# Linear-memory attention and MLP on one core: from a planner's order to a written list of tasks, with score quads in segment 0

## The chip, the cores and the metric

The kernel runs on one core of one Trainium2 chip. The metric is device time in microseconds (us) of one execution, as the median of several runs. The engines are TensorE (PE in the profile; its weight loads are PEld), VectorE (DVE), ScalarE (ACT), GpSimd (POOL) and SyncE (SP). SP issues all DMAs of this kernel. Each engine works through its own instructions in the order in which they are written down; semaphores make an instruction wait for results of other engines.

## What is computed

One transformer block over 2048 tokens of width 640: `x`, `LN` without gain or bias, attention in 4 segments of 512 tokens with a memory that is carried from segment to segment, a residual, a second `LN`, and an MLP of width 1728 with SiLU, with a residual.

```python
h  = x + attention(LN(x)) @ wo          # 32 heads of 20
h2 = h + silu(LN(h) @ w1) @ w2
# in attention, for each segment s and head:
p     = softmax(qs @ ks.T * scale + causal_mask)   # within the segment
a_mem = (phi(qs) @ M) / (phi(qs) @ z + 1e-6)       # phi(t) = t + 1 if t > 0 else exp(t)
o     = g * a_mem + (1 - g) * (p @ vs)             # g = sigmoid(beta)
M += phi(ks).T @ vs ; z += sum(phi(ks))
```

## The kernel before

The kernel is written as a graph of about 1300 tasks. A task is a small piece of work for one engine: the five matmuls of one projection, the evacuation of one result, one DMA. `Graph.task` notes what a task reads and writes, and `Graph.schedule` then decides in which order tasks are emitted, which engine takes those that ScalarE or VectorE could do, and which buffer each gets. It is a planner: it steps through a modelled time, and at each step gives each free engine the ready task with the lowest priority value. The priorities come from the table `P`. Where TensorE has no ready task, the planner puts in a filler, a matmul of zeros (L738). The `Tracker` then turns the emitted order into instructions with semaphore waits.

Per segment `s` (0 to 3) the tasks are these, with the lines of their instructions:

- Layer norm of 4 blocks of 128 tokens: statistics on VectorE (L841, L844), the reciprocal square root of the variance on POOL in two small steps (L850, L852), the normalisation on VectorE (L858). For the first four blocks TensorE transposes the result (L868), ScalarE or VectorE copies it to `nT` (L877, L878); all other blocks are transposed by a DMA (L883).
- V for 4 blocks (L910) and its evacuation (L920 on ScalarE, L921 on VectorE).
- Q and K as 5 chunks each (L938), evacuated to `QK` (L948 ScalarE, L949 VectorE). For the memory: the exponential of it (L956, ScalarE) and `phi` (L963, L966, VectorE). Chunks hold 4 heads per 32 partitions; 12 of the 32 heads are spread over the gaps of the chunks and are put together in `QKV` by 16 small DMAs (L977).
- The memory update from `phi(k)`, transposed by DMA (L1162), on TensorE (L1170), then VectorE or ScalarE (L1196, L1199) and POOL (L1206).
- 8 "ticks", each for a group of 4 heads: scores (L1018), exponentials (L1029, ScalarE, two banks per instruction), the causal mask on POOL (L1040), attention times V (L1068), its evacuation `oTs` (L1084, VectorE), the turn back to tokens and the memory's part (L1100, L1104), and the division (L1117 to L1137, VectorE; L1145, POOL).
- The back part: `otok` transposed by DMA (L1230), the product with `wo` (L1238), the residual (L1246), the second layer norm, 14 chunks of the hidden layer (L1266, and L1261 for the half chunk), SiLU by a tanh (L1280, ScalarE) and a product (L1285, VectorE), in segment 3 by one SiLU (L1274, ScalarE), the second product (L1326, L1301 for the last block), the second residual (L1336, L1311) and the output's DMA.

PSUM has two pools of four banks: `ps` (`ps_gen`) for nearly everything, `sc` (`ps_sc`) for scores. Scores use the array as four row tiles: the four heads of a group lie on 4 x 32 partitions, each with its own bank. There are 20 score groups per segment (per tick A and B, and one E for two ticks). `QUAD_SEGS` tells in which segments the four heads of a group are one task (a quad, all four `sc` banks); in the others they are two tasks of two heads (pairs, two banks each):

```python
QUAD_SEGS = (1, 2, 3)
for r0, nr in ([(0, 4)] if quad else [(0, 2), (2, 2)]):
    sca = G.alloc("sc", nr)
```

An exponential reads two banks, so a quad is read out by two of them and a pair by one. A `ps` buffer of two banks was always a neighbouring pair that begins at an even bank.

Of the kernel before, what the change touches and what calls it, by code (L numbers as in the profile page):

```python
# [210 lines left out]
class Alloc:  # L211
    __slots__ = ("pool", "size", "slot", "users", "last_write", "reads", "turn", "lock")

    def __init__(self, pool, size=1):
        self.pool = pool
        self.size = size
        self.slot = None
        self.users = 0
        self.lock = 0.0
        self.last_write = {}  # L220
        self.reads = {}

    def keys(self, subs):
        if self.pool in ("ps", "sc"):
            return [(self.pool, self.slot + i) for i in range(self.size)]
        return [(self.pool, self.slot, s) for s in subs]


class Task:
    __slots__ = ("name", "engs", "emit", "reads", "writes", "prio", "mode", "allocs", "preds", "npred",  # L230
                 "succ", "ready", "lat", "start", "end", "eng", "idx", "bw")
# [6 lines left out]
class Graph:  # L238
    def __init__(self, pools):
# [3 lines left out]
        self.flex = P["flex"]  # L243
        self.filler = None
        self.fill_from = 1.0
        self.start_at = 0.75
        self.fill_all = 12.0
        self.fill_to = 400.0
        self.free_order = ("x", "ps", "ex", "th", "st", "xn", "rd")

    def alloc(self, pool, size=1):
        a = Alloc(pool, size)
        a.turn = self.turns.get(pool, 0)
        self.turns[pool] = a.turn + 1
        return a

    def task(self, name, engs, emit, reads=(), writes=(), prio=0.0, mode=None, reserve=(), lat=None, bw=0.0):

        t = Task()
        t.name, t.engs, t.emit, t.prio, t.mode, t.lat, t.bw = name, engs, emit, prio, mode, lat, bw  # L260
# [31 lines left out]
    def schedule(self):  # L292
        import heapq
        tasks = self.tasks
        for t in tasks:
            t.succ = []
            t.npred = len(t.preds)
            t.ready = 0.0
            t.start = t.eng = None
        for t in tasks:  # L300
            for p in t.preds:
                tasks[p].succ.append(t.idx)
        free = {p: [True] * n for p, n in self.pools.items()}
        events = []
        engfree = {e: self.start_at for e in ENGS}
        pemode = [None]
        WIN = 3.4133
        busy = {}
        rate = {0: 0.5}

        def pe_rate(t):
            w = int(t / WIN)
            for v in range(max(rate), w):
                rate[v + 1] = 1.0 if busy.get(v, 0.0) >= 0.39 * WIN else 0.5
            return rate[w]

        def pe_busy(st, en, r):
            w = int(st / WIN)
            while st < en:
                e2 = min(en, (w + 1) * WIN)  # L320
                busy[w] = busy.get(w, 0.0) + (e2 - st) * r
                st = e2
                w += 1
        dmaq = [0.0]
        cand = {e: [] for e in ENGS}
        order = []
        left = len(tasks)

        def push(t):
            for e in t.engs:  # L330
                cand[e].append(t.idx)

        turn = {p: 0 for p in self.pools}

        def find(a):
            f = free[a.pool]
            if a.pool not in self.free_order and a.turn != turn[a.pool]:
                return None
            if a.size == 1:
                if a.pool == "ps":  # L340
                    n = len(f)
                    for i in range(n):
                        if f[i] and not f[i ^ 1]:
                            return i
                for i, x in enumerate(f):
                    if x:
                        return i
                return None
            for i in range(0, len(f), a.size):
                if all(f[i:i + a.size]):  # L350
                    return i
            return None

        def can(t):
            need = [a for a in t.allocs if a.slot is None]
            if not need:
                return True
            taken = []
            ok = True
            for a in need:  # L360
                i = find(a)
                if i is None:
                    ok = False
                    break
                for k in range(a.size):
                    free[a.pool][i + k] = False
                taken.append((a, i))
            for a, i in taken:
                for k in range(a.size):
                    free[a.pool][i + k] = True  # L370
            return ok

        def fill_ok(t):
            return t > self.fill_from and t < self.fill_to and (
                t < self.fill_all or busy.get(int(t / WIN), 0.0) < P["fill"] * WIN)

        now = self.start_at
        for t in tasks:
            if t.npred == 0:
                push(t)  # L380
        done_heap = []
        rel_heap = []
        while left:
            progressed = True
            hold = []
            while progressed:
                progressed = False
                for e in ENGS:
                    if engfree[e] > now + 1e-9:
                        continue  # L390
# [113 lines left out]
D = 640  # L504
# [892 lines left out]
```

## Time and profile before

| | |
|---|---|
| Median of 3 runs | 314.56 us (313.83 to 314.69) |
| Profiled execution | 313.93 us, of which 312.0 us span |
| TensorE busy | 300.4 us (96% of the span), 2719 matmuls |
| ScalarE busy | 212.0 us (68%) |
| VectorE busy | 220.2 us (71%) |
| POOL busy | 150.2 us (48%) |
| Granted TensorE clock | 1.00 throughout |

The span runs from the first to the last instruction of the program. "Busy" is the time in which at least one instruction of that engine is under way. A group's row gives line, engine, operation, what is written and read with shapes, the count, then busy time, the mean of one in ns, and the engine's idle time just before such instructions with what ended it. A chain's row gives start, length, engine, tile and line. A timeline's row gives start, length, engine, line, operation, shapes and count, and in brackets the idle time before it and who ended it. A stretch's row gives its bounds, its length, then the busy time of PE, PEld, DVE, ACT and POOL, each with a count of instructions, then the granted clock, DMA share and GB/s; for one line alone only the engines that it uses.

### The profile page before, as it was taken

To read this page: it belongs to the slowest core of one execution; us is meant where nothing else is said; L and a number is where in the kernel's file an instruction comes from. 1 tells how busy PE (TensorE), PEld (TensorE's weight loads), DVE (VectorE), ACT (ScalarE), POOL (GpSimd) and SP (SyncE) were. 2 spreads that over 40 slices of the span, in tenths; PEclk is the share of its full clock that TensorE was granted. 3 is DMA by queue.
4 is the path that set the end of the run, shared out by engine and by line. 5 is a ranking of instruction groups with operands and counts; after the bars stand their busy time and mean duration, and the time that the engine had idled before them with its cause. 6 is when DMAs were issued, how large, how long until landed. Compare 5 with 4: busy or idle time off the path is not lost.

```text
span 312.0 us, 6863 instructions
## 1 busy us (share of the span) xinstructions
PE 300.4 (96%) x2719; PEld 161.6 (52%) x2719; DVE 220.2 (71%) x454; ACT 212.0 (68%) x273; POOL 150.2 (48%) x292
## 2 busy tenths in 40 slices
PE   8999999988999999999999999999999999999996
PEld 6543543445644345565545454456654446664574
DVE  5649978895799889989897857993765695920012
ACT  2889999985669899878677678986568932005400
POOL 7879745652565546545476634654454431300000
PEclk9999999999999999999999999999999999999999
DMA  7657617755469300623150212332110004330001
GB/s 219 204 159 160 96 26 200 181 141 81 83 115 244 111 2 1 99 48 67 44 120 2 61 33 40 57 42 65 40 47 21 2 2 85 79 70 21 2 32 53
DMA packets 51103, 24.61 MB, mean 79 GB/s; under 512 B 39680, under 2 KB 49792, under 8 KB 51072
## 3 DMA queue, kind: packets, MB, share of 16 engines
q1 hardware_dynamic: 51072, 24.19, 34.9%
q8 instruction: 21, 0.34, 0.5%
q14 instruction: 10, 0.08, 0.1%
HBM read 10.41 MB, written 2.62 MB: 42 GB/s over the span
## 4 chain that ended last, share of the span: by engine, by line
PE 63%; DVE 14%; ACT 7%; POOL 5%; SPq 4%; DMA 4%; issue 3%; DVEq 0%; ACTq 0%
PE ps_gen L1326 17%; PE ps_gen L1266 10%; PE ps_gen L938 8%; PE ps_gen L1238 6%; PE ps_sc L1018 5%; PE ps_sc L1266 4%; PE ps_gen L1068 4%; SPq L977 3%; PE ps_gen L910 3%; ACT PTB L1029 3%; DVE on L1137 2%; DVE stt L841 2%; ACT PTA L1029 1%; DMA sT<-in_A_wq_dram 1%; PE ps_gen L1170 1%
## 5 line engine op out<-in xcount | busy, mean ns | idle before, releaser
L1029 ACT ACTIVATE PTA<-ps_sc 128x1024 bf16<-128x1024 f32 x64 | 63.0, 1033 | 14.9 <-PE ps_sc L1018 14.8
L1029 ACT ACTIVATE PTB<-ps_sc 128x1024 bf16<-128x1024 f32 x64 | 62.9, 1037 | 13.6 <-PE ps_sc L1018 13.5
L1326 PE MATMUL ps_gen<-w_sb,sT 128*128 128x320 bf16 x420 | 60.3, 299 | 0.3 <-DVE on L1137 0.3
L1040 POOL TENSOR_SCALAR_AFFINE_SELECT PTB<-PTB 128x512 bf16<-128x512 bf16 x64 | 41.5, 648 | 36.7 <-ACT PTB L1029 34.5
L1326 PEld LDWEIGHTS ps_gen<-w_sb,sT 128*128 128x128 bf16 x420 | 39.8, 98 | 18.5 <-issue 1.9
L1266 PE MATMUL ps_gen<-nT,w_sb 128*128 128x512 bf16 x195 | 46.7, 380 | 1.6 <-DVE sT L1285 1.4
L1029 ACT ACTIVATE PTE<-ps_sc 128x1024 bf16<-128x1024 f32 x32 | 31.1, 1031 | 8.3 <-PE ps_sc L1018 8.3
L1285 DVE SCALAR_TENSOR_TENSOR sT<-th,ps_gen 128x512 bf16<-128x512 f32 (+1 forms) x42 | 27.3, 661 | 10.7 <-ACT th L1280 10.2
L1040 POOL TENSOR_SCALAR_AFFINE_SELECT PTA<-PTA 128x512 bf16<-128x512 bf16 x32 | 21.0, 657 | 23.5 <-ACT PTA L1029 23.5
L1280 ACT ACTIVATE th<-ps_gen 128x512 f32<-128x512 f32 (+1 forms) x42 | 24.6, 593 | 10.1 <-PE ps_gen L1266 6.7
L1336 DVE SCALAR_TENSOR_TENSOR x_tok<-ps_gen,x_tok 128x640 bf16<-128x640 f32 x15 | 12.3, 820 | 24.6 <-PE ps_gen L1326 24.6
L841 DVE BATCH_NORM_STATS2 stt<-x_tok 128x6 f32<-128x320 bf16 x64 | 27.8, 476 | 2.4 <-DMA x_tok<-in_A_x_dram 2.3
L1266 PEld LDWEIGHTS ps_gen<-nT,w_sb 128*128 128x128 bf16 x195 | 17.4, 98 | 22.3 <-DVE sT L1285 3.2
L1040 POOL TENSOR_SCALAR_AFFINE_SELECT PTE<-PTE 128x512 bf16<-128x512 bf16 x32 | 20.6, 644 | 14.6 <-ACT PTE L1029 13.4
L949 DVE CAST QK<-ps_gen 128x512 bf16<-128x512 f32 x33 | 22.3, 680 | 7.5 <-PE ps_gen L938 7.5
L1145 POOL TENSOR_TENSOR otok<-on 128x320 bf16<-128x320 bf16 x24 | 19.2, 799 | 14.8 <-DVE on L1137 13.9
L1274 ACT ACTIVATE sT<-ps_sc 128x512 bf16<-128x512 f32 (+1 forms) x14 | 8.2, 582 | 26.6 <-PE ps_sc L1266 26.5
L1084 DVE TENSOR_SCALAR oTs<-ps_gen,lsc 128x512 bf16<-128x512 f32 x32 | 23.8, 743 | 3.4 <-PE ps_gen L1068 3.3
L938 PE MATMUL ps_gen<-nT,wqr 128*128 128x512 bf16 x100 | 25.0, 381 | 0.5 <-DVE QK L949 0.3
L938 PE MATMUL ps_gen<-nT,wkr 128*128 128x512 bf16 x100 | 25.0, 380 | 0.0
L910 PE MATMUL ps_gen<-wv_sb,nT 128*128 128x320 bf16 x160 | 24.1, 300 | 0.2 <-DVE on L1137 0.2
L1238 PE MATMUL ps_gen<-wo_sb,oT 128*128 128x320 bf16 x160 | 23.9, 299 | 0.4 <-DVE rd L1131 0.2
(98 smaller groups left out, 455.9 us busy)
## 6 DMA issues: line engine op xcount, KB each, us to landing
x_tok<-in_A_x_dram SPq DMA_DIRECT2D x16, 160.0 KB, 2.6
out_dram<-x_tok SPq DMA_DIRECT2D x15, 160.0 KB, 1.8
w_sb<-in_B_w_dram SPq DMA_DIRECT2D x5, 432.0 KB, 3.7
w_sb<-in_B_w_dram SPq DMA_DIRECT2D x6, 320.0 KB, 4.3
QKV<-QK SPq DMA_DIRECT2D x16, 72.0 KB
sT<-in_A_wq_dram SPq DMA_DIRECT2D x2, 400.0 KB, 5.1
sT<-in_A_wk_dram SPq DMA_DIRECT2D x2, 400.0 KB, 5.7
wv_sb<-in_A_wv_dram SPq DMA_DIRECT2D x1, 800.0 KB, 7.8
```

Of the source, the lines that this page charges most:

```text
L841: T.add(DV, lambda e, hh=hh: e.bn_stats(out=stt[:, s, 6 * hh:6 * hh + 6], in_=xb[:, 320 * hh:320 * hh + 320]), reads=R((xa, xsub)), writes ...
L910: fns.append(lambda e, c=c, hh=hh: e.matmul(bank(ps, hh)[:, 0:320], lhsT=xT[:, c, 128 * i:128 * i + 128], rhs=wv_sb[:, c, :].rearrange("p ...
L938: fns = [lambda e, kc=kc: e.matmul(bank(ps), lhsT=wt[:, kc, c, :], rhs=xT[:, kc, :], start=(kc == 0), stop=(kc == NC - 1)) for kc in range ...
L949: (lambda e: e.tensor_copy(out=o, in_=bank(ps)))
L1029: T.add(AC, lambda e: e.activation(out=pt[:, pta.slot, q0:q0 + 2, :], in_=sc3[:, b0:b0 + 2, :], func=ACT.Exp, scale=SCALE), reads=[("sc", ...
L1040: fns.append(lambda e, v=v: e.affine_select(out=v, in_=v, pattern=[[0, 4], [1, 128]], compare_op=ALU.is_ge, fill=0.0, base=0, channel_mult ...
L1084: f = lambda e: e.tensor_scalar(out=oTs[:, ots.slot, :], in0=bank(po), scalar1=lsc[:, g:g + 1], scalar2=None, op0=ALU.mult)
L1238: fns.append(lambda e, c=c, hh=hh: e.matmul(bank(ps, hh)[:, 0:320], lhsT=oT[:, c, 128 * i:128 * i + 128], rhs=wo_sb[:, c, 320 * hh:320 * h ...
L1266: fns = [lambda e, c=c: e.matmul(bank(ps), lhsT=w1_sb[:, c, 128 * f:128 * f + 128], rhs=hT[:, c, :], start=(c == 0), stop=(c == NC - 1)) f ...
L1280: T.add(AC, lambda e: e.activation(out=th[:, tha.slot, 0:nt], in_=bank(ps)[:, 0:nt], func=ACT.Tanh, scale=0.5), reads=R((ps, [0])), writes ...
L1285: T.add(DV, lambda e: e.scalar_tensor_tensor(out=sT[:, f, 0:nt], in0=th[:, tha.slot, 0:nt], scalar=1.0, in1=bank(ps)[:, 0:nt], op0=ALU.add ...
L1326: fns.append(lambda e, f=f, hh=hh: e.matmul(bank(ps, hh)[:, 0:320], lhsT=s_of(i, f), rhs=w2_of(i, f, 320 * hh), start=(f == 0), stop=(f == ...
```

## The change

- The planner is gone. `ORDER` lists all 1313 tasks by number in the order in which they are placed, `ENGINE` gives each task's engine by a letter, and `BANK` the first `ps` bank of each result. `schedule` places them one after the other at the earliest time its model allows, takes other buffers as they come free, and sorts by start. The order on each engine is therefore another one throughout, SP's too.
- Fillers are put in only before 12 us of the modelled time, and only while TensorE waits there.
- Segment 0 is in `QUAD_SEGS`: its scores are quads like the others.
- Two-bank results that are evacuated through `pair` (V, `wo`, the second product, L1100/L1104) may lie in any two banks, also not neighbours.
- In the first layer norm of the first four blocks, the statistics of block 1 come from ScalarE: one pass that copies the block and sums it, one that squares its distance from the mean and sums that, each followed by a small product with 1/640 on POOL. The other three stay on VectorE.
- The reciprocal square root of these four blocks is taken for two blocks at a time (POOL, 128x2 in place of 128x1), and their normalisations follow it.
- The load of the first weights: K's half before Q's. Blocks 8 to 11 of `x` are loaded early.
- In the order of the whole, ScalarE does 11 of the 32 `oTs` evacuations (none before) and 11 of the 40 `QK` evacuations (7 before).

The diff, cut to its core:

```diff
-QUAD_SEGS = (1, 2, 3)
+QUAD_SEGS = (0, 1, 2, 3)
 NPE = 2
 TP_SC = (1, 2)
+ST_ACT = (1,)
...
+ORDER = [
+    51, 47, 0, 1, 49, 113, 50, 46, 48, 114, 115, 116, 112, 3, 2, 125, 5, 124, 117, 118, 119, 4, 121, 122, 7, 120, 126,
...
+ENGINE = (
+    "sssssssssssssssssssssssssssssssgssssssssssssssgggggdgggdagddadgdgggggggggggggggggggggggggggggdgdgada"
...
+BANK = (
+    "0200022113320210200133110120332021100222010001003121033002202210213030021313310101222202203230202020"
...
     def schedule(self):
-        import heapq
         tasks = self.tasks
...
+        for idx in ORDER:
+            t = tasks[idx]
+            e = t.eng
+            st = free[e]
+            for p in t.preds:
+                p = tasks[p]
+                st = max(st, p.end if e == PE and p.eng == PE else p.ready)
...
+            if e == PE:
+                if st < self.fill_all:
+                    fill(max(free[PE], self.fill_from), st)
...
+        order.sort(key=lambda t: t.start)
...
     def pair(a):
-        return flat(a).rearrange("p (b x) -> p b x", b=2)
+        i, j = a.banks
+        return ps_all[:, :].rearrange("p (b x) -> p b x", b=4)[:, i:j + 1:j - i, :]
...
+        def e_sum(eng):
+            s = st.slot + j
+            T.add(AC, lambda e: e.activation(out=xn_rot[:, xn.slot, :], in_=x_tok[:, b, :], func=ACT.Identity,
+                                             accum_out=stt[:, s, 0:1]),
+                  reads=R((xa, xsub)), writes=R((st, [f"s0{j}"]), (xn, [0])))
+
+        def e_sq(eng):
+            s = st.slot + j
+            T.add(AC, lambda e: e.activation(out=xn_rot[:, xn.slot, :], in_=x_tok[:, b, :], func=ACT.Square,
+                                             scale=-1.0, bias=mvt[:, s, 0:1], accum_out=stt[:, s, 1:2]),
+                  reads=R((xa, xsub), (st, [f"m{j}"])), writes=R((st, [f"s1{j}"]), (xn, [0])))
...
+        if early and b in ST_ACT:
+            G.task(f"{tag}sa{b}", {AC: act_c(640) + 0.1}, e_sum, [(xa, xsub)], [(st, [f"s0{j}"]), (xn, [0])], prio)
+            part("sm", 0, f"m{j}")
+            G.task(f"{tag}sq{b}", {AC: act_c(640) + 0.1}, e_sq, [(xa, xsub), (st, [f"m{j}"])],
+                   [(st, [f"s1{j}"]), (xn, [0])], prio)
+            part("sv", 1, f"v{j}")
...
         def e_rstd(eng):
-            s = st.slot
-            T.add(PO, lambda e: e.tensor_tensor(out=rst[:, s, :], in0=mvt[:, s, 1:2], in1=eps_c[:, 0:1], op=ALU.add),
-                  reads=R((st, ["mv"]), (C, ["eps"])), writes=R((st, ["r"])))
...
+            r, v = rst[:, st.slot:st.slot + n, 0], mvt[:, st.slot:st.slot + n, 1]
+            T.add(PO, lambda e: e.tensor_tensor(out=r, in0=v, in1=eps_c[:, 0:1].to_broadcast([128, n]), op=ALU.add),
+                  reads=R((st, vs), (C, ["eps"])), writes=R((st, ["r"])))
```

More of the change, by code (lines that the diff above doesn't have):

```diff
@@ L325, in schedule @@
[L325 to L352, printed above, removed]
@@ new lines, in schedule @@
+        banks = iter(BANK)
+        for t, e in zip(tasks, ENGINE):
+            t.eng = dict(p=PE, a=AC, d=DV, g=PO, s=SP)[e]
+            for a in t.allocs:
+                if a.pool == "ps" and a.banks is None:
+                    i = int(next(banks))
+                    a.banks = list(range(i, i + a.size))
+        order = []
+        rel = {p: [0.0] * n for p, n in self.pools.items()}
+        held = {p: [False] * n for p, n in self.pools.items()}
+        turn = {p: 0 for p in self.pools}
```

388 lines of the change are left out of this document (175 added, 213 removed), and 71 rows, old and new, of tables (ORDER, P).

## The prediction

> **What bounds the kernel now.** I read the page first (engine totals, then the chain that ended last), then stretches, then single instructions.
>
> ```profile
> PE 300.4 (96%) x2719; PEld 161.6 (52%) x2719; DVE 220.2 (71%) x454; ACT 212.0 (68%) x273; POOL 150.2 (48%) x292
> ...
> PE 63%; DVE 14%; ACT 7%; POOL 5%; SPq 4%; DMA 4%; issue 3%; DVEq 0%; ACTq 0%
> ```
>
> TensorE is the bound, yet "96%" does not mean that nothing is left. A matmul's recorded time includes its way through the array, which overlaps the next one. So I count from start to start, with prices from the chain in order of time:
>
> ```profile
> 48.14 1.08 PE ps_gen L938 x5
> 49.22 0.32 PE ps_sc L1018 x2
> 49.54 1.19 PE ps_gen L938 x5
> 50.72 0.46 PE ps_sc L1018 x6
> 51.19 1.19 PE ps_gen L938 x5
> 52.37 0.32 PE ps_sc L1018 x4
> 52.69 0.66 PE ps_gen L1068 x16
> ...
> 267.91 11.41 PE ps_gen L1326 x84
> 279.32 1.73 PE ps_sc L1266 x8
> ```
>
> A 512-column matmul takes 0.216 us (1.08 / 5, 1.73 / 8) and a 320-column one 0.136 (11.41 / 84). Five matmuls that end in a change of array shape, from full to row-tiled scores (L1018), take 1.19 instead of 1.08, so a change costs about 0.1 us.
>
> ```profile
> 11.06 1.24 PE L938 MATMUL ps_gen<-nT,wkr 128*128 128x512 bf16 x5
> ```
>
> Segment 0 runs from this first projection (11.06) to the first score of segment 1 (66.73); the rest goes to the end of the last matmul.
>
> ```profile
> 11.03:66.72 55.69, 54.53 (x475) 25.16 (x473) 43.61 (x105) 52.96 (x72) 38.98 (x91) 1.00 0.59 139
> 66.72:309.41 242.69, 236.83 (x2178) 129.78 (x2177) 168.37 (x330) 153.98 (x194) 102.23 (x172) 1.00 0.28 57
> ```
>
> The columns are length, then busy time of PE, PEld, DVE, ACT, POOL. In segment 0 ScalarE (52.96 of 55.69) is as full as TensorE; later TensorE stands alone (ACT 153.98 of 242.69). Counting the rest at the prices above: 360 matmuls of 512 columns 77.8, 688 of 320 columns 93.6, 292 small ones 14.5, 25 groups of L1068, 60 of scores and 4 half-wide, with their changes of shape, 45.5. The largest groups of that stretch are
>
> ```profile
> L1326 PE MATMUL ps_gen<-w_sb,sT 128*128 128x320 bf16 x420 | 60.3, 299 | 0.3 <-DVE on L1137 0.3
> L1266 PE MATMUL ps_gen<-nT,w_sb 128*128 128x512 bf16 x195 | 46.7, 380 | 1.6 <-DVE sT L1285 1.4
> ```
>
> That is 231.4 us of work in 242.7: TensorE waits some 11.3 us there (13 filler matmuls lie inside). The same count of segment 0 gives 53.6 us of work and 2.1 of waits.
>
> **The change, part by part.** The build's order has the same real matmuls, 17 fewer fillers (46, none after the start) and 202 changes of array shape instead of 219.
>
> *Scores of segment 0 by quads.* Before, each of its 20 score groups is two pairs, mostly with other work between; afterwards one quad.
>
> ```profile
> 14.60:66.72 52.12, 12.85 (x128) 3.93 (x128) 1.00 0.61 142
> 66.72:247.20 180.48, 23.76 (x384) 6.68 (x384) 1.00 0.31 62
> ```
>
> These are the L1018 instructions alone. Segments 1 to 3 need 23.76 / 60 = 0.396 us per group, so 20 groups would be 7.9 busy instead of 12.85. Part of the 4.9 is array delay that the next matmul hides; from start to start it is 8.1 against 4.7, a gain of 3.4, which I take (bounds 3 to 4.9). The 17 fewer changes of shape give 17 x 0.1 = 1.6 to 1.7. Sum of both: -5.0.
>
> *What the quad costs.* A quad fills all four score banks, so the next cannot start before both exponentials of this one are read out. The tightest such loop, on PE and then on ACT:
>
> ```profile
> 164.26 0.29 PE L1018 MATMUL ps_sc<-QK 20*128 20x256 bf16 x4
> 164.38 0.28 PE L1018 MATMUL ps_sc<-QKV 20*128 20x256 bf16 x4
> 164.59 1.53 PE L1238 MATMUL ps_gen<-wo_sb,oT 128*128 128x320 bf16 x10
> 165.96 0.33 PE L1100 MATMUL ps_gen<-Mzb,phiQ 128*128 128x96 bf16 x4
> 166.13 0.33 PE L1104 MATMUL ps_gen<-sel,oTs 128*128 128x96 bf16 x4
> 166.70 0.40 PE L1018 MATMUL ps_sc<-QKV 20*128 20x512 bf16 x4 [0.24 <-ACT PTE L1029]
> ```
>
> ```profile
> 140.48 1.67 ACT L956 ACTIVATE ex<-QK 128x512 bf16<-128x512 bf16 x3
> ...
> 164.71 1.94 ACT L1029 ACTIVATE PTE<-ps_sc 128x1024 bf16<-128x1024 f32 x2 [0.68 <-PE ps_sc L1018]
> 167.15 1.02 ACT L1029 ACTIVATE PTA<-ps_sc 128x1024 bf16<-128x1024 f32 x1 [0.50 <-PE ps_sc L1018]
> ```
>
> From quad to quad at least 2.44 us pass (164.26 to 166.70). I summed what TensorE has between consecutive quads of the new segment 0: in 11 of 20 places less than that, 22.7 us together where 11 x 2.44 = 26.8 are needed. So TensorE waits 4.2 us there for ScalarE. One more ACT instruction per loop (0.52: three L956 end 1.67 after the first begins, one alone takes 0.63) fits the 0.5 us in which ACT waits for the scores; one place has three, 0.3 more. The Trainium skill ("TensorEngine Tiling (Array Packing)", Gotcha 1: PSUM Pressure) says that different row tiles write to different PSUM banks. By that rule a quad must take four, and the loop agrees: the quad at 166.70 starts 0.05 us after ACT has left the banks.
>
> *The start.* On VectorE before:
>
> ```profile
> 7.06 0.21 DVE L844 BATCH_NORM_AGGREGATE mvt<-stt 128x2 f32<-128x12 f32 x1
> 7.21 1.31 DVE L858 TENSOR_SCALAR xn_rot<-x_tok,mvt,rst 128x640 bf16<-128x640 bf16 x3
> 8.45 0.19 DVE L753 TENSOR_SCALAR sel<-iot 128x96 bf16<-128x96 int32 x1
> 8.79 0.71 DVE L858 TENSOR_SCALAR xn_rot<-x_tok,mvt,rst 128x640 bf16<-128x640 bf16 x1 [0.15 <-POOL rst L852]
> 9.42 0.81 DVE L878 CAST nT<-ps_sc 128x640 bf16<-128x640 f32 x1
> 10.15 0.81 DVE L878 CAST nT<-ps_gen 128x640 bf16<-128x640 f32 x1
> ```
>
> Statistics of four blocks end at 7.27, the last normalisation (behind POOL's rstd) at 9.50, the last copy at 10.96, and the first projection follows at 11.06. With block 1 on ScalarE, VectorE has its three blocks done about 1.0 earlier, and the second pair's rstd should be out near 7.6. Four normalisations of 0.44 then end near 8.6, one weight copy and one L878 near 9.9; first projection about 10.1. I take -1.0 (bounds -0.3, if block 1's two ACT passes and four small POOL steps come late, and -1.4). The new list then has the first score right after both projections, where before V work stood between: TensorE must wait 0.7 for the evacuation.
>
> *Segment 0 together.* Work 53.6 becomes 49.65 (scores -3.4, 14 fewer changes of shape -1.35, three memory products pulled in, one small step moved out). From 10.1: 49.65 + 0.7 + 4.2 + 0.3 + 0.7 for other waits = 65.6, where before stood 66.73. So -1.1: the quads nearly pay for themselves in waits.
>
> *The rest.* Work falls by 1.1 (what segment 0 pulled in, three changes fewer). Of the 11.3 of waits, some 2.9 stand at 66.7 to 74.6, around the end of segment 0, ending with
>
> ```profile
> 74.57 0.50 PE L1170 MATMUL ps_gen<-Vx,phiKt 128*128 128x192 bf16 x4 [1.04 <-DMA phiKt<-phiK]
> ```
>
> That transpose was issued on SP behind seven L977 copies; in the new SP order it stands ahead of all of segment 1's. Most of the other 8.4 end with a VectorE evacuation. The new list gives ScalarE 11 of the 32
>
> ```profile
> L1084 DVE TENSOR_SCALAR oTs<-ps_gen,lsc 128x512 bf16<-128x512 f32 x32 | 23.8, 743 | 3.4 <-PE ps_gen L1068 3.3
> ```
>
> and four more L949 copies, some 11 us off VectorE. Bounds: all of 8.4 stay or grow by half (rigid lists can hold an evacuation behind something late), or nearly all go. I take 4.7. New ones: 1.2 where TensorE's work between quads is under 2.44 (segment 3), and 0.9 before the last segment's first product: before, three blocks' second product (the 11.41 row) covered layer norm and transposes there, now two (7.6). Waits 11.3 -> 6.8, so -4.5, and with the work -5.6.
>
> *Sum.* The profiled execution took 313.93 (span 312.0 and 1.93 around it; the median of the runs is 0.63 above). 313.93 - 1.1 - 5.6 = 307.2; I say 307.0. The same by parts: start -1.0, work -5.0, waits 13.4 -> 12.7.
>
> **Rivals.**
> *The waits do not shrink.* The fixed list only shifts them and the VectorE part stays at 8.4: 307 + 3.7 = 310.7; with half as much again 315. For: the distance from the last attention output product to the next segment's first hidden product shrinks to 7 or 8 us of TensorE work everywhere. Against: less VectorE load. Chance 0.2, of it 0.05 at no change.
> *The quad loop decides (slower).* Place: segment 0's loop on ScalarE. The 24 other ACT instructions between its exponentials hide in no gap: 24 x 0.52 = 12.5 on 20 x 2.44 = 48.8, the first exponential at about 13.5, so segment 1 starts near 75 instead of 65.6, and the kernel takes 316. It decides from about 0.29 us exposed per instruction. For: ACT has 52.96 of 55.69 there already. Against: the row at 167.15, where ACT idled 0.50 inside the loop. By that page of the Trainium skill (Gotcha 1: PSUM Pressure) taken alone the result would be this one, since a quad that takes a bank for each row tile has no second buffer here. Chance 0.09, and 0.05 for a late list elsewhere that gives the same.
> *The loop waits cost nothing extra.* The 4.2 absorb other waits and VectorE is quick: 302 to 303. Chance 0.1.
>
> **How the numbers follow.** Forecast (303 to 310.5) 0.56, the rivals as given. A difference under 0.3% (0.9 us) can't be told from none here. Faster: 0.56 + 0.1 + 0.15 = 0.81; same 0.05; slower 0.14. The range 301 to 315 leaves out part of the slow rivals and the lowest waits.
>
> **What would show it.** Right: L1018 busy near 7.9 in segment 0, ACT's loop there near 2.44 to 2.6 per quad with TensorE waiting there for the exponentials, first projection near 10.1, segment 1's first score near 65.6, fewer TensorE waits on VectorE later. Wrong: first exponential later than 15, segment 1's first score after 68, or TensorE waits over 13 us after it, above all on LN chains and DMA transposes.

## The result and the profile after

The changed kernel takes 312.20 us (median of 15 runs, 310.33 to 316.14) where the kernel before takes 314.55 (15 runs, 313.83 to 315.48): a ratio of 0.9926 with a 95% interval of 0.9902 to 0.9950. Run again on another chip, beside the kernel before, it took 312.47 us, ratio 0.9938 (0.9913 to 0.9962). So it is faster by some 2 us, less than a third of the 7 us forecast. The ratios leave out single runs over 1.5% above their kernel's fastest (316.14 here, one each in two of the variants below), the medians do not.

The profiled execution took 312.17 us, of which 310.3 are span. First the engine totals and the chain by engine, from the changed kernel's page:

```profile
PE 291.9 (94%) x2674; PEld 159.4 (51%) x2702; DVE 214.1 (69%) x435; ACT 223.5 (72%) x291; POOL 150.0 (48%) x293
...
PE 67%; ACT 12%; DVE 9%; DMA 6%; issue 3%; SPq 1%; POOL 0%; POOLq 0%; ACTq 0%; DVEq 0%
```

The 291.9 are too low: 28 matmuls lack a record (2674 of 2702; the weight loads are complete, and all 28 have 512 columns). With these put back TensorE is busy about 295.5 us, 5.0 us less than before (300.4), and that is still 95% of the span, which is only 1.7 us shorter. ScalarE's place on the chain grows from 7% to 12%, VectorE's falls from 14% to 9%. Nine of the profiles told of here, this one among them, lack such records, and in all nine the first matmul of the first projection is one of them. Times of the first projection and waits are given below with these matmuls put back, counted from start to start at 0.216 us each; recorded rows are shown as they are.

Now the two stretches, cut at the first recorded matmul of the first projection (the real first one began at 11.62) and at segment 1's first score, columns as before:

```profile
11.82:69.18 57.36, 50.53 (x473) 24.86 (x478) 48.55 (x109) 51.91 (x69) 41.65 (x101) 0.99 0.57 130
69.18:307.70 238.52, 231.77 (x2136) 127.66 (x2156) 158.67 (x310) 166.28 (x214) 102.41 (x172) 0.99 0.29 60
```

Segment 0 became longer, 57.6 (from 11.62) for 55.7, although TensorE, with the matmuls put back, is busy about 3.0 us less in it; the rest became 4.2 us shorter. The scores of segment 0 alone (L1052, before L1018):

```profile
14.60:69.18 54.58, 7.92 (x128) 2.26 (x128) 0.99 0.55 120
```

7.92 busy for 12.85: as forecast. The start, from the timeline:

```profile
3.08 0.89 DVE L828 BATCH_NORM_STATS2 stt<-x_tok 128x6 f32<-128x320 bf16 x2 [2.02 <-DMA x_tok<-in_A_x_dram]
5.71 0.89 DVE L828 BATCH_NORM_STATS2 stt<-x_tok 128x6 f32<-128x320 bf16 x2 [1.49 <-DMA x_tok<-in_A_x_dram]
9.09 1.21 DVE L878 TENSOR_SCALAR xn_rot<-x_tok,mvt,rst 128x640 bf16<-128x640 bf16 x2 [0.59 <-POOL rst L870]
11.61 0.33 PEld L971 LDWEIGHTS ps_gen<-nT,wkr 128*128 128x128 bf16 x3 [0.20 <-ACT nT L900]
11.84 0.38 PE L971 MATMUL ps_gen<-nT,wkr 128*128 128x512 bf16 x1
```

VectorE stands idle for 1.49 us until the third block of `x` has landed. The row at 11.84 is the first projection's second matmul; the first, whose weights are loaded at 11.61, left no record, so the projection comes at about 11.62. In segment 0 two places stand out. Around 50 us (SP's rows are the issues of DMAs):

```profile
45.07 0.44 SPq L651 DMA_DIRECT2D w_sb<-in_B_w_dram  x1
45.56 1.20 SPq L1196 DMA_TRANSPOSE phiKt<-phiK  x1
46.81 0.59 SPq L651 DMA_DIRECT2D w_sb<-in_B_w_dram  x1
47.44 1.19 SPq L1196 DMA_TRANSPOSE phiKt<-phiK  x1
...
52.62 0.66 PE L1204 MATMUL ps_gen<-Vx,phiKt 128*128 128x288 bf16 x4 [1.36 <-DMA phiKt<-phiK]
```

The memory product of chunk 3 waits for a transpose issued 5.2 us earlier, right behind a weight load of 432 KB. And at the segment's end:

```profile
65.48 0.90 DVE L878 TENSOR_SCALAR xn_rot<-x_tok,mvt,rst 128x640 bf16<-128x640 bf16 x1
66.30 0.34 DVE L1233 TENSOR_TENSOR Mz<-ps_gen,Mz 128x192 f32<-128x192 f32 x1
66.70 0.40 PE L1102 MATMUL ps_gen<-PTA,Vx 128*32 128x512 bf16 x4 [0.75 <-DVE Mz L1233]
67.53 0.49 DVE L1153 TENSOR_TENSOR otok<-ps_gen,rd 128x320 bf16<-128x320 f32 x1
68.17 0.77 PE L1204 MATMUL ps_gen<-Vx,phiKt 128*128 128x192 bf16 x4 [0.74 <-DVE otok L1153]
69.19 0.61 PE L1052 MATMUL ps_sc<-QK 20*128 20x512 bf16 x4
```

TensorE waits twice for PSUM banks that VectorE empties late, the first time behind a layer-norm apply ("apply" is the normalisation of one block, L878). Right after, its clock is halved; a stretch of the changed kernel, clock in the third column from the end:

```profile
68.22:71.63 3.41, 3.41 (x28) 1.89 (x32) 2.18 (x6) 2.67 (x4) 2.00 (x3) 0.50 0.58 131
```

Last, the largest wait of the rest, near 92 us:

```profile
91.89 0.45 DVE L878 TENSOR_SCALAR xn_rot<-x_tok,mvt,rst 128x640 bf16<-128x640 bf16 x1 [1.35 <-DMA nT<-xn_rot]
92.25 0.69 DVE L982 CAST QK<-ps_gen 128x512 bf16<-128x512 f32 x1
...
92.99 0.34 PE L1134 MATMUL ps_gen<-Mzb,phiQ 128*128 128x96 bf16 x4 [1.16 <-DVE QK L982]
```

VectorE itself stands still for 1.35 us in an apply, whose buffer a transpose is still reading; the evacuation of a `QK` tile is queued behind it, and TensorE waits for that tile's bank.

### The profile page after: what moved, and what is told of

Same layout as the page of the kernel before. It is cut to its first block, busy times and chain, and to the rows that moved or that the text cites. A ratio compares the mean times of both kernels' runs of the same rounds, so it can differ in the third digit from the quotient of the medians.

```text
span 310.3 us, 6823 instructions
## 1 busy us (share of the span) xinstructions
PE 291.9 (94%) x2674; PEld 159.4 (51%) x2702; DVE 214.1 (69%) x435; ACT 223.5 (72%) x291; POOL 150.0 (48%) x293
## 4 chain that ended last, share of the span: by engine, by line
PE 67%; ACT 12%; DVE 9%; DMA 6%; issue 3%; SPq 1%; POOL 0%; POOLq 0%; ACTq 0%; DVEq 0%
PE ps_gen L1360 16%; PE ps_gen L971 10%; PE ps_gen L1300 9%; PE ps_sc L1052 6%; PE ps_gen L943 5%; PE ps_gen L1102 5%; PE ps_sc L1300 4%; PE ps_gen L1272 4%; ACT PTB L1063 4%; ACT PTA L1063 3%; ACT th L1314 2%; DMA nT<-xn_rot 2%; PE ps_gen L1134 2%; DVE stt L828 2%; PE ps_gen L1204 2%
## 5 line engine op out<-in xcount | busy, mean ns | idle before, releaser
L1063 ACT ACTIVATE PTB<-ps_sc 128x1024 bf16<-128x1024 f32 x64 | 62.1, 1022 | 9.4 <-PE ps_sc L1052 9.2
L1360 PE MATMUL ps_gen<-w_sb,sT 128*128 128x320 bf16 x420 | 61.4, 299 | 0.6 <-DVE x_tok L1280 0.6
L1300 PE MATMUL ps_gen<-nT,w_sb 128*128 128x512 bf16 x185 | 45.1, 380 | 1.3 <-DVE sT L1319 0.5
L828 DVE BATCH_NORM_STATS2 stt<-x_tok 128x6 f32<-128x320 bf16 x62 | 27.0, 477 | 3.8 <-DMA x_tok<-in_A_x_dram 3.5
L982 DVE CAST QK<-ps_gen 128x512 bf16<-128x512 f32 x29 | 19.8, 684 | 7.9 <-PE ps_gen L971 7.9
L971 PE MATMUL ps_gen<-nT,wkr 128*128 128x512 bf16 x93 | 23.2, 379 | 1.0 <-issue 0.8
L971 PE MATMUL ps_gen<-nT,wqr 128*128 128x512 bf16 x91 | 22.8, 379 | 1.1 <-issue 0.7
L1370 DVE SCALAR_TENSOR_TENSOR x_tok<-ps_gen,x_tok 128x640 bf16<-128x640 f32 x15 | 12.4, 824 | 16.1 <-PE ps_gen L1360 15.8
L1052 PE MATMUL ps_sc<-QK 20*128 20x256 bf16 (+3 forms) x320 | 20.4, 304 | 2.4 <-ACT PTA L1063 1.1
```

The source lines that it names most:

```text
L828: T.add(DV, lambda e, hh=hh: e.bn_stats(out=stt[:, s, 6 * hh:6 * hh + 6], in_=xb[:, 320 * hh:320 * hh + 320]), reads=R((xa, xsub)), writes ...
L971: fns = [lambda e, kc=kc: e.matmul(bank(ps), lhsT=wt[:, kc, c, :], rhs=xT[:, kc, :], start=(kc == 0), stop=(kc == NC - 1)) for kc in range ...
L982: (lambda e: e.tensor_copy(out=o, in_=bank(ps)))
L1052: fns.append(lambda e, j=j, o=o, n=n, r=r, qa=qa, ka=ka: e.matmul(sc_all[:, o:o + n], lhsT=ka[32 * r:32 * r + DH, 128 * j:128 * j + 128], ...
L1063: T.add(AC, lambda e: e.activation(out=pt[:, pta.slot, q0:q0 + 2, :], in_=sc3[:, b0:b0 + 2, :], func=ACT.Exp, scale=SCALE), reads=[("sc", ...
L1300: fns = [lambda e, c=c: e.matmul(bank(ps), lhsT=w1_sb[:, c, 128 * f:128 * f + 128], rhs=hT[:, c, :], start=(c == 0), stop=(c == NC - 1)) f ...
```

## The experiments

The table gives each one's median, its ratio to the kernel before on the same chip, and from its profile: first projection; from there to segment 1's first score; from there to the end of the last matmul. (The expectations go by the recorded 11.84 and 57.35 of the changed kernel, which are 11.62 and 57.57 here.) Line numbers in the rows of some variants are 1 or 3 higher than in the changed kernel.

| kernel | us | ratio (95%) | start | segment 0 | rest |
|---|---|---|---|---|---|
| before | 314.55 | 1 | 11.06 | 55.67 | 242.60 |
| changed | 312.20 | 0.9926 (0.9902 to 0.9950) | 11.62 | 57.57 | 238.43 |
| changed, again | 312.47 | 0.9938 (0.9913 to 0.9962) | 11.26 | 58.45 | 239.57 |
| two loads behind transposes | 308.03 | 0.9807 (0.9784 to 0.9829) | 10.82 | 57.76 | 235.84 |
| LN apply later | 310.49 | 0.9870 (0.9834 to 0.9905) | 10.81 | 57.15 | 238.84 |
| pairs in segment 0 | 310.94 | 0.9888 (0.9868 to 0.9909) | 10.45 | 58.72 | 237.77 |
| statistics on VectorE | 310.54 | 0.9868 (0.9847 to 0.9890) | 10.95 | 56.99 | 238.00 |
| evacuation first | 309.66 | 0.9848 (0.9821 to 0.9875) | 11.09 | 56.94 | 236.29 |
| three loads behind transposes | 308.89 | 0.9831 (0.9810 to 0.9852) | 11.08 | 58.02 | 236.39 |
| three moves together | 310.63 | 0.9878 (0.9858 to 0.9897) | 10.39 | 56.33 | 238.95 |
| load order of before | 311.25 | 0.9898 (0.9874 to 0.9921) | 11.31 | 57.22 | 237.52 |
| loads spread, two moves | 308.29 | 0.9796 (0.9767 to 0.9825) | 10.64 | 55.34 | 236.40 |
| the same with pairs | 308.54 | 0.9791 (0.9760 to 0.9823) | 11.12 | 54.48 | 236.85 |
| rstd one block at a time | 311.19 | 0.9899 (0.9872 to 0.9925) | 11.12 | 56.73 | 239.29 |
| beta ahead of the weights | 312.46 | 0.9946 (0.9916 to 0.9976) | 13.86 | 59.21 | 236.95 |

The theory after reading the trace: three kinds of waits ate the gain, each with its own cause (SP's order, VectorE's order, the loads at the start). The rival: the quad loop paces segment 0, so that a wait removed comes back elsewhere.

**The changed kernel once more**, no edit.

> The changed kernel itself once more, on the chip that the next three use, as their yardstick. Theory (its first profile fell on a late landing of the third block of x and on the half-clock stretch, both by chance): the third block lands before 5.2 us, the first projection comes at 10.8 and not at 11.84, and the median is 310.5 to 312.2, above the run with kt03 first (308.0) by 2 us or more. Rival (the late landing belongs to the order of the loads): the third block lands at 5.5 or later again and the first projection comes at 11.5 or later.

Measured: VectorE's second pair of statistics starts at 5.27, the first projection at 11.26, median 312.47. Neither expectation fits fully: landing and start lie between them, the start nearer to the rival. Two rows of its timeline, around 50 us and around 230 us, tell how much the same program moves from execution to execution:

```profile
53.57 0.67 PE L1204 MATMUL ps_gen<-Vx,phiKt 128*128 128x288 bf16 x4 [2.20 <-DMA phiKt<-phiK]
```

```profile
233.34 1.02 PE L1300 MATMUL ps_gen<-nT,w_sb 128*128 128x512 bf16 x4 [1.72 <-DMA nT<-xn_rot]
```

The first is the wait of 1.36 from above; the second has no counterpart in the first profile (there 0.1 us). This one, for the last layer-norm transpose ahead of segment 2's hidden layer, was 1.7 to 2.0 us from start to start in 4 of 13 profiles of changed kernels and at most 0.5 in the other 9.

**Two weight loads behind the transposes.**

```diff
 L651 load of w_sb, 432 KB
 L1196 transpose of phiK, chunk 2
-L651 load of w_sb, 432 KB
 L1196 transpose of phiK, chunk 3
-L651 load of w_sb, 320 KB
 L1196 transpose of phiK, chunk 4
+L651 load of w_sb, 432 KB
+L651 load of w_sb, 320 KB
```

> The changed kernel with two weight loads of the feed-forward moved on SyncE behind the transposes of phiK of chunks 3 and 4 (nothing else). Theory (the wait was real loss): the memory product of chunk 3, which stood idle 1.36 us for its transpose in the changed kernel's trace (50.87 to 52.57), waits under 0.3 us, segment 1's first score comes at 67.8 instead of 69.19, and the time falls by 1.4 us to 310.8 (ratio to the kernel before 0.988). Rival (the quad loop paces segment 0): the idle time turns up before the next score tile, segment 1's first score stays within 0.3 us of 69.2, and the time stays at 312.2 (0.9926).

Measured: 308.03 us, the fastest median of all, but not for the reason given. Its timeline around 50 us:

```profile
45.70 7.37 SPq L1196 DMA_TRANSPOSE phiKt<-phiK  x3
...
51.27 0.50 PE L1204 MATMUL ps_gen<-Vx,phiKt 128*128 128x192 bf16 x4 [1.37 <-DMA phiKt<-phiK]
```

Now chunk 2's product waits 1.37 us, and segment 0 is no shorter (57.76). What was gained lies elsewhere: a start at 10.82, no half clock, and no wait near 90 us (from segment 1's third tick to its fourth 7.98 us instead of 9.21). The last came by accident: VectorE has no wait of its own in the apply there. The likely reason, not shown, is that the moved loads shifted the modelled times by which `place` takes buffers, so that this apply got a buffer that nobody was reading.

**The evacuation ahead of the waiting apply**, which does the same on purpose.

```diff
-L878 apply (waits for a transpose to have read its buffer)
 L982 evacuation of segment 2's first QK tile
+L878 apply
```

> The changed kernel with one VectorE instruction moved: the evacuation of segment 2's first QK tile (L982) ahead of the LN apply that waits for a transpose to have read its buffer. Theory (the wait of 1.23 to 1.55 us before L1134 at 90 to 92 us, released by that evacuation, is VectorE's order): it falls below 0.2 us and the time falls by 1.2 to 1.5 against the changed kernel run beside it. Rival (the LN apply, now later, delays the transposed blocks and the work that reads them): the wait is gone but its time turns up within the next 40 us and the time stays within 0.4 us.

Its timeline near 89 us:

```profile
88.79 0.69 DVE L982 CAST QK<-ps_gen 128x512 bf16<-128x512 f32 x1 [0.28 <-PE ps_gen L971]
...
89.67 0.34 PE L1134 MATMUL ps_gen<-Mzb,phiQ 128*128 128x96 bf16 x4
```

L1134 no longer waits, and that step takes 7.98 us. The time fell by 2.8 us against the changed kernel beside it (309.66 to 312.47), more than the 1.2 to 1.5 that this wait explains. The part beyond that isn't shown to be the edit's: the profile with the edit also drew smaller waits at 50 us (0.83) and 230 us (0.1), and full clock.

**The LN apply of block 9 later.**

```diff
-L878 apply of block 9
 L1233 memory add; L1151, L1153 normalisation; L1151, L1153 normalisation
+L878 apply of block 9
```

> The changed kernel with one VectorE instruction moved: the LN apply of block 9 (0.90 us at 65.48) stands behind the memory add and the two normalisations that TensorE waits for (L1233, twice L1151 and L1153), instead of ahead of them. Theory (VectorE's order makes the waits at the end of segment 0, and these the half clock): the waits of 0.75 and 0.74 us before L1102 at 66.70 and L1204 at 68.17 fall below 0.4 us together, the half-clock stretch of 3.41 us goes or shrinks, the mean clock is 1.000, and the time falls by 1.1 for the waits and by up to 1.7 for the clock, to 309.4 to 311.1, with a smaller spread. Rival (another release is next in line): the waits move to the memory products of chunks 2 and 3, segment 1's first score stays at 69.2, and the time is 312.2.

Its timeline at the end of segment 0:

```profile
65.33 0.34 DVE L1233 TENSOR_TENSOR Mz<-ps_gen,Mz 128x192 f32<-128x192 f32 x1
65.73 0.40 PE L1102 MATMUL ps_gen<-PTA,Vx 128*32 128x512 bf16 x4
...
66.57 0.49 DVE L1153 TENSOR_TENSOR otok<-ps_gen,rd 128x320 bf16<-128x320 f32 x1
67.20 0.49 PE L1204 MATMUL ps_gen<-Vx,phiKt 128*128 128x192 bf16 x4 [0.74 <-DVE otok L1153]
```

The first of the two waits is gone, the second is as long as it was: half of the expectation. The clock was 1.000 in 5 of 6 runs. The time fell by 1.7 to 2.0 us, of which 0.75 is the wait. The rest can't be put down to the edit: the variant with VectorE's statistics, which keeps both waits, came out at 310.54 too.

**Three loads behind the transposes.**

```diff
-L651 load of w_sb, 432 KB
 L1196 transpose of phiK, chunk 2
-L651 load of w_sb, 432 KB
 L1196 transpose of phiK, chunk 3
-L651 load of w_sb, 320 KB
 L1196 transpose of phiK, chunk 4
+L651 load of w_sb, 432 KB
+L651 load of w_sb, 432 KB
+L651 load of w_sb, 320 KB
```

> The changed kernel with three weight loads of the feed-forward (432, 432 and 320 KB) moved on SyncE behind the transposes of phiK of chunks 2 to 4. In the run that moved two of them, the memory products waited 1.44 us all the same, with the first load still ahead. Theory (the loads ahead slow the transposes): without any load ahead the transpose of chunk 2 lands within 3 us of its issue, the wait before L1204 at 50 us falls below 0.4 us, and segment 0 (first projection to segment 1's first score, 57.35 us in the changed kernel's trace) shortens by 1 us or more. Rival (the transposes come too late since SyncE's 16 copies to QKV, 0.65 to 0.69 us each, end at 45.2, and two transposes share the queues): the wait stays above 1 us.

Its timeline from 51 us on:

```profile
51.11 1.53 SPq L651 DMA_DIRECT2D w_sb<-in_B_w_dram  x3
...
58.77 1.27 SPq L1196 DMA_TRANSPOSE phiKt<-phiK  x1
...
59.80 0.50 PE L1204 MATMUL ps_gen<-Vx,phiKt 128*128 128x192 bf16 x4 [1.84 <-DMA phiKt<-phiK]
```

The wait at 50 us is gone, so the loads ahead had made it. But the three loads now stand ahead of the next chunk's transpose, and its product waits 1.84 us. Segment 0 gains nothing (58.02); in this profile the clock is also at half from 61.01 to 64.42, behind that wait.

**The three moves together** (the three loads, the apply of block 9, the evacuation).

> The three moves together: the three weight loads behind the transposes, the LN apply of block 9 behind the normalisations, and segment 2's first evacuation ahead of the LN apply. Theory (the waits are independent): the gains add up to 4 to 5 us against the changed kernel run beside it, 306 to 307.5 (ratio to before 0.974 to 0.980), and the clock stays at 1.000. Rival (the quad loop of 2.45 to 2.5 us paces segment 0 and only the later move counts): 309 to 310.

Measured: 310.63, outside of both. Segment 0 fell to 56.33, with a wait of 1.5 us left behind the three loads, and the rest drew the wait near 230 us (1.7). Only 4 runs; why it stands above its parts isn't settled.

**The loads spread, with the two VectorE moves.** One load behind the transpose of block 8, one ahead of that of block 10, three behind the transposes of `otok`.

> The changed kernel with the weight loads taken off every transpose of phiK of segment 0: one of 432 KB behind the transpose of block 8, one where another stood before block 10, three behind the transposes of otok; and the two VectorE moves of the runs before. Theory (each wait in the first 92 us has its own cause, and the sum of three moves failed since the loads were put ahead of the next chunk's transposes): no wait for a transpose of phiK over 0.5 us is left, segment 1's first score comes 54.5 to 55.5 us after the first projection (57.35 in the changed kernel, 56.1 with the three moves), and the time is 306.5 to 308.5. Rival (the loads only move the wait on again): another wait of 1.5 to 2 us for a transpose appears between 80 and 110 us and the time is 309 to 310.5.

No product waits for a transpose of `phiK` any more, segment 0 takes 55.34, and the time is 308.29: as expected, and with the next kernel the best ratio of all. It beats the changed kernel by 1.3% and the kernel before by 2.0%.

**Pairs in segment 0**, once in the changed kernel and once in the one just told.

```diff
-QUAD_SEGS = (0, 1, 2, 3)
+QUAD_SEGS = (1, 2, 3)
```

with the second pair of each group in `ORDER` right behind the first.

> The changed kernel with segment 0's scores by pairs again: each quad is two pairs, one right behind the other in the quad's place, so that no shape change is added; all else is the same. Theory (quads save TensorE time as the prediction had it, and the loop costs a part of it): TensorE's work grows by 2.5 to 3.4 us, the waits of segment 0 shrink by 1 to 1.5 because the first exponential starts half a tile earlier, and the time is 313.5 to 315 (0.996 to 1.001). Rival (the quad loop of 2.45 us paces segment 0 and eats the saving): segment 1's first score comes no later than 69.2 and the time is 311 to 312.5.

> The kernel of the run beside it (loads spread, two VectorE moves) with segment 0's scores by pairs, one pair right behind the other in the quad's place. Theory (quads are worth their TensorE work, 1.2 us for 4.67 against 5.86 us of score products, and no more, since the exponentials pace the loop either way): the time is 0.8 to 1.6 us above the run beside it. Rival (the earlier first exponential pays for the work): equal within 0.5 us or faster.

The first came out at 310.94 (ratio 0.9888), below both expectations and not slower than the changed kernel; its segment 0 was long (58.72), with the wait at 50 us and a half clock from 53.39 to 56.80 in it, and its start early, so it can't decide. The second can, since the waits for transposes are out of the way. The stretch of segment 0, columns as before and both cut at the first recorded matmul, first of the kernel with quads:

```profile
10.85:65.97 55.12, 50.09 (x473) 24.60 (x478) 47.67 (x108) 50.85 (x68) 40.92 (x99) 1.00 0.48 114
```

and of the same with pairs:

```profile
11.33:65.59 54.26, 51.25 (x473) 25.38 (x478) 48.27 (x108) 50.20 (x68) 40.84 (x99) 1.00 0.49 114
```

With pairs TensorE is busy 1.2 us longer, and the segment is 0.9 us shorter. Counted from start to start, score work is 6.09 instead of 4.67, and the waits for exponentials are 0.87 instead of 2.96. The times are equal (308.54 and 308.29). So the rival holds: in this order quads are worth nothing that could be measured over adjacent pairs. ScalarE is busy 50 to 51 of 54 to 55 us in either, which fits a segment that it paces; but TensorE is as full, so that isn't shown.

**Statistics of block 1 on VectorE** (`ST_ACT = ()`), **rstd one block at a time, the load order of before.**

```diff
-ST_ACT = (1,)
+ST_ACT = ()
```

> The changed kernel with the LN statistics of block 1 back on VectorE (between those of blocks 0 and 3); the pairs for rstd and the load order stay. Theory (the late start came from the late landing of the third block, 5.69 us, which is chance of the loads): the first projection comes at 10.9 to 12.0 depending on that landing alone, no earlier than with ScalarE's statistics at the same landing, and the time is within 0.5 us of 312.2. Rival (statistics by ScalarE are what made the start late, by the accumulator reads and the extra products): with VectorE's statistics the first projection comes at 10.9 or earlier also with a late landing, and the time falls by 0.8 to 311.4.

> The changed kernel with rstd of blocks 0 to 3 one block at a time again (four pairs of GpSimd instructions of 128x1 instead of two of 128x2); statistics by ScalarE, load order and the number of fill products stay. Theory (a pair waits for the later of its two blocks): rstd of block 3 is ready 1 us earlier, its apply and transposes run ahead of those of block 2, and the first projection comes 0.2 to 0.5 us earlier at the same landing of x (that is at the landing of the third block's statistics plus 5.7, against plus 6.1 in four of the traces so far); the time falls by as much. Rival (GpSimd's extra starts cost as much): the first projection comes no earlier than landing plus 6.0.

> The changed kernel with the first eight loads in the order of the kernel before (blocks 0, 1, 2, 3 of x, then w_q ahead of w_k in both halves), VectorE's statistics of blocks 2 and 3 in that order, and no more fill products than the changed kernel has. In the trace of before the packets of the four blocks had ended at 4.44 us, in six traces with the changed order at 4.86 to 5.99. Theory (the order makes the weights' packets overtake the last of x): the four blocks have landed by 4.6, the first projection comes at 10.0 to 10.6, and the time falls by 0.7 to 1.2 against the changed kernel (312.2 to 312.5). Rival (chance of the queues): they end at 4.8 or later again, the first projection comes at 10.8 to 11.8, the time is unchanged.

With all statistics on VectorE, those of its first three blocks run without a gap (its timeline), and the first projection comes at 10.95:

```profile
3.07 0.89 DVE L828 BATCH_NORM_STATS2 stt<-x_tok 128x6 f32<-128x320 bf16 x2 [2.00 <-DMA x_tok<-in_A_x_dram]
4.12 0.83 DVE L828 BATCH_NORM_STATS2 stt<-x_tok 128x6 f32<-128x320 bf16 x2
5.11 0.83 DVE L828 BATCH_NORM_STATS2 stt<-x_tok 128x6 f32<-128x320 bf16 x2
```

VectorE does block 1 in the time that it otherwise waits for the third block. In the 11 profiles with ScalarE's statistics and paired rstd the first projection lies at 10.39 to 11.62 (mean 10.96), some 5.6 to 6.3 us behind the start of the third block's statistics. Rstd by single blocks gave 5.7 where eight of those eleven gave 5.8 to 6.3: the pair costs perhaps 0.2 us. The load order of before did not land `x` earlier (last packet at 5.50, first projection 11.31): chance, not the order. All three times (310.54, 311.19, 311.25) lie 1 to 2 us below the changed kernel's, more than their starts (10.95, 11.12, 11.31) account for; that part isn't explained.

**The kernel before, two more profiles, and beta ahead of the weights.**

> The kernel before once more, for its trace. Theory (the loads of x land later in the changed kernel by something the change did): the packets of the four blocks of x have ended by 4.5 us again (4.44 in its first trace; 4.86 to 5.99 in ten traces of changed kernels, the one with before's load order among them), and the first projection comes at 11.0. Rival (chance): they end at 4.8 or later and the first projection comes at 11.3 or later.

> The same kernel as in the look before it, for a second draw, with the same expectations: packets of x ended by 4.5 us (theory) or at 4.8 us or later (chance).

> The kernel with the loads spread and the two VectorE moves (308.29 us, ratio 0.9796), with the two loads of beta ahead of the first weight load on SyncE, so that the weights are issued 0.9 to 1.8 us later. Theory (weight packets overtake the last packets of x, which end at 5.29 there, and the start hangs on those): the blocks of x have landed by 4.5, the first projection comes at 9.9 to 10.4 instead of 10.86, and the time falls by 0.5 to 0.9 to 307.4 to 307.8. Rival (the weights, now later, take over as what the first projection waits for): the first projection comes at 10.8 or later and the time does not fall.

The packets of `x` ended at 5.37 and 5.55 us and the first projection came at 11.50 and 11.27. Chance: the trace that the prediction was made from had drawn an early landing (4.44). By the trace's records of single packets 52 weight packets went ahead of the last packet of `x` there, and 110 to 547 in the others. The Trainium skill ("DMA: Bandwidth & Descriptors", Queues, rings and completion order) says that a DMA is split over up to 16 engines, whose data may complete out of order; these counts agree.

Beta ahead of the weights kept them back, as wanted (no weight packet before the last of `x`, at 4.63), but at a price, as its timeline shows:

```profile
2.67 0.94 SPq L667 DMA_DIRECT2D beta_bc<-in_A_beta_dram  x2
3.65 0.47 SPq L654 DMA_DIRECT2D sT<-in_A_wk_dram  x1
...
4.74 3.01 SPq L654 DMA_DIRECT2D sT<-in_A_wk_dram  x1
7.79 3.76 SPq L654 DMA_DIRECT2D sT<-in_A_wq_dram  x1
...
13.86 2.29 PE L974 MATMUL ps_gen<-nT,wkr 128*128 128x512 bf16 x5 [4.44 <-DVE nT L904]
```

Two loads of 4 KB hold up the second half of the weights' issues (3.01 and 3.76 us; 0.53 and 1.61 in the changed kernel), the weights come 4 us later and the clock is halved for 10.24 us. The rival holds, by far: 312.46.

## Why the prediction was right and wrong

It forecast 307.2 for an execution that took 312.17. The direction held, and so did the outer range of 301 to 315; the size did not, and the time lies outside the forecast's own band of 303 to 310.5. Stage by stage the misses are start +1.5, segment 0 +2.1, rest +1.4, together 5.0. Of its signs of being wrong one came: segment 1's first score after 68 (69.19).

- *TensorE's work, -5.0*: right to 0.3. Score groups in segment 0 fell from 8.09 to 4.68 from start to start, changes of shape from 219 to 202; segment 0's work measured 49.4 to 49.7, by how the changes of shape are priced, for a forecast of 49.65. But the credit to "quads" was wrong: adjacent pairs keep 2.0 to 2.2 of the 3.4, and all of the saved changes of shape.
- *The start, -1.0*: the step that failed is "VectorE has its three blocks done about 1.0 earlier". It took the landings of one trace as fixed. Three profiles of before start at 11.06, 11.50 and 11.27, eleven of changed kernels at 10.96 in the mean: a gain of about 0.3, since VectorE waits for the third block in the time won.
- *Segment 0, waits of 5.9*: measured some 8, from other sources. For the exponentials 2.6, where 4.2 + 0.3 were forecast: the loop of 2.45 to 2.5 us was met, but other waits fell into the same places. For the `QK` evacuation 0.8 (0.7 forecast). "0.7 for other waits" is the term that failed: 1.5 for a transpose behind a weight load, 0.4 for `QKV`, 1.6 for VectorE at the end, hence 3.5, and some 1 in small waits. The forecast had asked what the quads wait for, and not what the new order of SP and VectorE puts in front of a release.
- *The rest, -5.6*: 4.2 measured. Waits that end with VectorE fell to between 4.0 and 4.9 (4.7 forecast), the new one of 1.23 near 92 us, for an apply with a buffer still being read, among them. The wait before the last segment's first hidden product was there, 0.47 for 0.9. What the forecast had no term for is about 0.9 of half clock after 69 us and 0.5 for a transpose of `otok` at 83.8; without the wait near 92 the VectorE term would have come out better than forecast.
- *The clock*: not in the prediction at all, a term put at nothing. In both profiles of the changed kernel the half-clock stretch made the way from segment 0's last tick to segment 1's second 16.1 us long, where the four variants with the same order there and full clock took 14.8: 1.3 us. Over whole runs that drowns: the 14 runs with a mean clock of 0.994 or 0.995 average 312.45, the 7 with 1.000 average 312.04.
- *Rivals*: "the waits do not shrink" (310.7) came closest in time, but by luck: the VectorE waits that it kept at 8.4 did shrink. "The loop waits cost nothing extra" was wrong: 2.6 us of waits for exponentials stood in segment 0. "The quad loop decides (slower)" was wrong in size, but right in its premise, that quads leave ScalarE without a second buffer. The Trainium skill ("TensorEngine Tiling (Array Packing)", Gotcha 1: PSUM Pressure) states that row tiles take a bank each; the pair run shows its price here, 2.1 us of waits.

What stays open: how much of the last 1 to 2 us of any single variant is its edit and how much a draw. Five variants with quite different edits (apply later, pairs, VectorE's statistics, load order, single rstd) all lie at 310.5 to 311.3. Making the start independent of the draw, and the waits of 0.76 and 0.47 us near 269 and 277 us, wasn't tried.

## What to carry to other kernels

When a change replaces the whole order, count what stands in front of each late release on each in-order engine, SP's DMA queue first: moving five loads and two VectorE instructions took 4 us off here (1 to 2 of them may be a draw), and undoing quads, ScalarE's statistics or paired rstd cost nothing that could be measured. A saving on an engine can come back as waits in a stage where another engine is as full; do the cheaper half of it (here pairs next to each other) and measure. And take a landing time from one trace as a draw, not as a constant.

## What the runs showed of the hardware

- In both profiles of the changed kernel the clock fell to half for 3.41 us right after two waits of 0.75 us within 2.2 us. The waits alone don't bring it: in five profiles of variants (pairs, VectorE's statistics, evacuation first, load order, single rstd) the same two waits stand at the same place, and the clock stayed full behind them. The Trainium skill ("TensorE: Matmul & The Clock Gate", Why this matters for your kernels) warns of idle gaps over some 3 us; by that rule none of these waits would have mattered, so here the measurement decides. The Trainium skill tells in the same page's section "A second HAM failure mode: psum-queue depth-cycling" of short idle times that do it, and that agrees better.
- In the five traces in which the clock fell twice, the two falls lie a whole multiple of 3.413 us apart (68.22 and 310.57: 71 of them). Counted on that beat, TensorE was idle for 1.5 to 1.84 us of the stretch of 3.41 us just before each of four half clocks (1.73 and 1.5 in the two profiles of the changed kernel, 1.73 in that of pairs, 1.84 in that of three loads). Four other stretches with 1.5 to 1.66 us idle were not followed by one, and none with 1.41 or less was. In the three of the five profiles with full clock where the beat can be told, it parts the two waits. So what seems to count is the idle time that falls into one stretch, and where a stretch begins is a draw; no run tests it.
- A sum taken along by ScalarE costs an extra read of 0.19 us per pass, as an instruction of its own behind the 0.74 and 0.83 us of the pass.
- A DMA transpose of `phiK` took 2.3 to 6.0 us from issue to landing. Those of chunks 2 and 3 took 3.6 and 5.1 us behind a weight load each (changed kernel), and 2.4 each with no load ahead (three loads behind transposes).
- Two loads of 4 KB, in packets of 16 bytes, ahead of loads of 400 KB made the issues of the third and fourth of these take 3.01 and 3.76 us instead of 0.53 and 1.61.
